# Last pair's token transform: two products over the whole array in place of four on its quarters

## The chip, the core and the metric

The kernel runs on one core of one Trainium2 chip. The metric is the device time of one execution in microseconds (us), the median of several runs. The profiler records one execution; its times are counted from the start of the recorded span.

## What is computed

The input `x` has 2048 tokens of 512 channels. It is normalised over the channels; a spectral filter (a two-dimensional transform, a product with complex weights, the transform back) gives `s`; a token-mixing network (two matrix products over the token axis with a GELU between) and a SiLU give the gate `g`; the result is `x + s * g`.

```
xn = layernorm(x)
s = irfft2(rfft2(xn) * (w_r + 1j * w_i))
u = gelu(einsum("bsd,sf->bdf", xn, w1) + b1)
y = einsum("bdf,fs->bds", u, w2) + b2
return x + s * silu(y.transpose(0, 2, 1))
```

## The kernel before

The tokens are laid out as 128 rows times 16 row blocks. The kernel first normalises, transforms forward, multiplies by the spectral weights and makes the hidden products `h` by `w1` (up to about 200 us); then it runs a loop over `p = 0..7`, each step making the output of two row blocks, `p` and `p + 8`, a *pair*. All of what is described here lies in that loop, and most of it in its last step, `p = 7`.

In a step the tensor engine (PE) makes seven groups of 21 products of 128x128 weights by 256 columns, `products(p, n)` for `n` in `ORDER = (1, 2, 5, 6, 3, 7, 4)`; their left factors are `fa`, `fb`, `fc`, `fd` and their right factors the tiles `w2f`, which ACT and DVE form ahead of time from the loaded tiles `a` and `s`. The sums of the groups lie in PSUM banks 2 to 5. ACT turns them into gates `g`: `gate(g0, ...)` for the first row block, `gate(g1, ...)` for the second. The last group, `n = 4`, completes the left half of the second gate.

Beside that, the transform back over the channels runs on PE (`even_channels`, `odd_channels`, the products of `cd` by `yt`), DVE and ACT fold its output in `unfolded` (tiles `es`, then `y`), and `spectral(p)` makes the transform back over the tokens: `y` (128 rows; two halves of 512 columns, one for each row block) times constants of `cft`, into PSUM banks 0 and 1. It writes

```
for e, cols in enumerate((slice(0, 64), slice(64, P))):
    for r, rows in enumerate((slice(0, 64), slice(64, P))):
        i = e ^ r
        T.matmul(ps[cols, i], cft[rows, cols], y[rows, i], ...)
```

that is, four products of 64 rows by 64 columns of weights, each with 512 moving columns, on the four quarters of the array. They are in plain float32, and every one of them has two records in the trace. The other large products take rounded float32 (`F32R` in the code; the rows call both `f32`) and have one record each.

For `p < 7` the token transform of a pair is run in the next step, among other products. For the last pair it stands in that pair's own step, between `products(7, 7)` and `products(7, 4)` (`k == 5`). Then `finish` multiplies the banks by the gates (DVE, tile `rows`), adds `x` (tile `xr`, loaded earlier) and sends the rows out: `finish(g0, j0, whole)` for the first row block, `finish(g1, j1, right_)` for the right half of the second, and, when the last gate is there, `finish(g1, j1, left_)` in two parts.

Every operation of this loop is recorded by the wrapper `Kept`, so the profile gives them all the same line, L139; they are told apart by their tiles. In this part of the program the engines run their instructions in the order of the code. SP's queue issues the loads; an issue that has to wait for a semaphore holds up those behind it.

Of the kernel before, what the change touches and what calls it, by code (L numbers as in the profile page):

```python
# [9 lines left out]
F32 = mybir.dt.float32  # L10
# [5 lines left out]
P = 128  # L16
# [32 lines left out]
def _k1(lo, hi):  # L49

    (t, h), s = divmod(hi, 2), 2 * lo + hi // 2
    return (64 - s if s else 32) if h else s


def _pairs(lo, t):


    if 2 * lo + t == 0:
        return np.array([[1, 0, 1, 0], [1, 0, -1, 0], [0, 1, 0, 0], [0, 0, 0, 1]], float)
    return np.array([[1, 0, 1, 0], [0, 1, 0, 1], [1, 0, -1, 0], [0, -1, 0, 1]], float)  # L60


def _constants():


    q = np.arange(P)
    a = 2 * np.pi * (np.outer(q, np.arange(32)) % P) / P
    f = np.stack([np.cos(a), np.sin(a)], 2)
    f[0::2, 0, 1], f[1::2, 0, 1] = np.cos(np.pi * q[0::2] / 2), np.sin(np.pi * q[1::2] / 2)
    f = np.concatenate([f[0::2], f[1::2]]).reshape(P, 64)  # L70

    a = 2 * np.pi * (np.outer(2 * np.arange(P) + 1, KD) % (2 * D)) / (2 * D)
    fd = np.stack([np.cos(a), -np.sin(a)])
    fd[1, :, 0] = np.cos(np.pi * np.arange(P))
    fd = fd.reshape(2, P, 2, P).transpose(0, 2, 1, 3).reshape(4, P, P)
    iv = fd.transpose(0, 2, 1) * 2.0 / (D * S)
    iv[0, 0] *= 0.5
    iv[2, 0] *= 0.5  # L80

    g = np.zeros((P, 8, 2, 32, 2))
    back = np.zeros((8, 2, P, 2, 64))
    freq = np.zeros((P, 8, 2), int)
    j = np.arange(16)
    for lo in range(16):
        for hi in range(4):
            k1, (n, l), (t, h) = _k1(lo, hi), divmod(lo, 2), divmod(hi, 2)
            for r in range(16):
                rows = cr, sr = np.arange(16) * 2 + hi * 32, np.arange(16) * 2 + hi * 32 + 1  # L90
                out = np.zeros((2, P))
                if k1:
                    k = [k1 + 128 * r] * 2
                    th = 2 * np.pi * ((j * k[0]) % S) / S
                    out[0, cr], out[0, sr] = np.cos(th), -np.sin(th)
                    out[1, cr], out[1, sr] = -np.sin(th), -np.cos(th)
                elif r == 0:
                    k = [0, S // 2]
                    out[0, cr], out[1, cr] = 1.0, np.cos(np.pi * j)
                else:  # L100
                    k = [128 * r if r < 8 else 64 + 128 * (r - 8)] * 2
                    th = 2 * np.pi * ((j * k[0]) % S) / S
                    out[0, rows[r >= 8]], out[1, rows[r >= 8]] = np.cos(th), -np.sin(th)
                rows = slice(64 * t, 64 * t + 64)

                out[:, rows] = np.einsum("sajb,abhc->shjc", out[:, rows].reshape(2, 2, 16, 2),
                                         _pairs(lo, t).reshape(2, 2, 2, 2)).reshape(2, 64)
                p = [l * 64 + 2 * (h * 16 + r) + c for c in range(2)]
                for s in range(2):
                    g[rows, n, l, h * 16 + r, s] = back[n, t, p[s], 0] = out[s, rows]  # L110
                    freq[p[s], n, t] = k[s]
                if k[0] == k[1]:
                    back[n, t, p[0], 1], back[n, t, p[1], 1] = -out[1, rows], out[0, rows]
                else:
                    back[n, t, p, 1] = out[:, rows]
    freq = freq.reshape(P, 16)


    ft = np.concatenate([np.concatenate([f[:64].T, f[64:].T], 1)] * 2)
    c = {  # L120
        "c_f": f.astype(np.float32),
        "c_ft": np.concatenate([ft, np.array([-1.0, -2.0]) * np.where(q % 2, -1.0, 1.0)[:, None]], 1).astype(np.float32),
        "c_d": fd.transpose(1, 0, 2).astype(np.float32),
        "c_i": iv.transpose(1, 0, 2).astype(np.float32),
        "c_g": g.transpose(1, 0, 2, 3, 4).astype(np.float32),
        "c_h": back.transpose(0, 2, 1, 3, 4).astype(np.float32),
    }
    return c, freq
# [10 lines left out]
        return lambda *args, **kw: self.keep(operation(*args, **kw))  # L139


def spectral_mixer_kernel(tc, x, w1, b1, w2, b2, wk, we, wx, c_f, c_ft, c_d, c_i, c_g, c_h, out):
    nc = tc.nc
    V, A, G, T, SY = nc.vector, nc.scalar, nc.gpsimd, nc.tensor, nc.sync

# [16 lines left out]
    with tc.tile_pool(name="ps", bufs=1, space=PSUM) as psp, ExitStack() as left, ExitStack() as right:  # L162
        ps = psp.tile([P, 8, 512], F32, name="ps")
# [297 lines left out]
        T = Kept(T, keep)  # L461
# [46 lines left out]
        for j in range(NJ):  # L508
# [25 lines left out]
            start, more_stats = j < 3, j + 3 < NJ  # L534
# [38 lines left out]
            if more:  # L573
# [3 lines left out]
                if FIRST <= j < FIRST + NE:  # L577
                    i = j - FIRST
# [206 lines left out]
        for n in range(8):  # L785
            a, b, c, d, e, f = PACE[n]
# [115 lines left out]
        def banks(p):  # L902
            return ps[:, 2 + p % 2, :HD], ps[:, 4, :HD], ps[:, 5, :HD]
# [33 lines left out]
        V, A, SY, G = (Kept(e, keep) for e in (nc.vector, nc.scalar, nc.sync, nc.gpsimd))  # L937
        fp = pool(left, "left", "fin", 1)
# [67 lines left out]
        def spectral(p):  # L1006

            y = ys.pop(p)
            for e, cols in enumerate((slice(0, 64), slice(64, P))):
                for r, rows in enumerate((slice(0, 64), slice(64, P))):  # L1010
                    i = e ^ r
                    T.matmul(ps[cols, i], cft[rows, cols], y[rows, i], start=True, stop=True)

        def gate(g, j, cols, src, scale):
            A.activation(g[:, cols], src, AF.Silu, bias=b2t[:, j:j + 1], scale=scale)

# [18 lines left out]
        yts, ys, pieces = {}, {}, iter(())  # L1035
        last_rows = None

        for p in range(NP):
            j0, j1 = p, p + NP
            more = p + 1 < NP  # L1040
            if p:
                gates[p] = new_gates(p)
            g0, g1 = gates[p]
            bx, by, bz = banks(p)
            slot, plan = SLOTS[min(p, 2) + (not more)]
            gathering = gathered(p)
            for k, n in enumerate(ORDER):
                started = not p and k < 2
                if not started:
                    products(p, n)  # L1050
                if n == 1 and p:
                    p1 = copied(f"p1_{p}", bx, w2p)
                elif n == 5:
                    p5 = copied(f"p5_{p}", bz, fp)
                elif n == 6:
                    v2 = copied(f"v2_{p}", bx, fp)
                elif n == 7:
                    c22 = summed(f"c22_{p}", bx, p5)
                if not started:
                    ready.extend(w for w in [next(wforms, None)] if w is not None)  # L1060
                if n == 2:
                    c11 = summed(f"c11_{p}", by, p1)
                elif n == 6:
                    gate(g0, j0, left_, c11, 1.0)
                elif n == 3:
                    gate(g0, j0, right_, summed(f"c12_{p}", bz, v2), 1.0)
                elif n == 7:
                    gate(g1, j1, right_, c22, -1.0)
                elif n == 4:
                    for cols in (left_,) if more else quarter_rows:  # L1070
                        gate(g1, j1, cols, bx[:, cols], -1.0)
                if not p and k == slot - 1:
                    even_channels(p)
                if k == slot:
                    for part in PARTS[p]:
                        {"S": spectral, "E": even_channels, "O": odd_channels}[part](p - (part == "S"))
                    yts.pop(p)
                    pieces = unfolded(p)
                    if p:
                        for g, j in zip(gates.pop(p - 1), (j0 - 1, j1 - 1)):  # L1080
                            finish(g, j, whole)
                for what in plan.get(k, ""):
                    next(gathering if what == "g" else pieces)
                if more and n == 7:
                    sums_of_blocks()
                if not more and k == 2:
                    xr = [where.tile([P, NH * P], F32, name=f"xr{i}", tag="s1", bufs=1)[:, :D] for i, where in enumerate((w2p, fp))]
                    for to, j in zip(xr, (j0, j1)):
                        for rows, tokens in halved:
                            SY.dma_start(to[rows], x[tokens, j])  # L1090
                if not more and k == 5:
                    spectral(p)
                    last_rows = fp.tile([P, 2, D], F32, name="rows", tag="yt")
                    finish(g0, j0, whole)
                    finish(g1, j1, right_)
# [38 lines left out]
```

## Time and profile before

| | us |
|---|---|
| median of 3 runs | 366.15 |
| lowest and highest of them | 365.76, 366.25 |
| the profiled execution: its own time | 366.07 |
| the profiled execution: its span, first to last instruction | 364.3 |
| PE busy, share of the span | 357.4, 98% |
| DVE busy, share of the span | 306.4, 84% |
| ACT busy, share of the span | 211.1, 58% |
| granted TensorE clock, mean | 0.999 of full speed |

The profiled execution takes 1.8 us more than its span. A row of the timeline gives the start, the length, the engine and the tiles (out<-in) of instructions that are merged into one row where they are alike and follow each other, with their count. PE is the matmul stream, PEld the weight loads, which can run beside it. The ends of matmuls are modelled, and they overlap: what one costs the stream is read from start to start.

### The profile page before, as it was taken

Reading aid. Unit: us, or ns where it says so; the run is one execution under the profiler, and the core shown is the slowest. Engines: PE = TensorE matmul, PEld = TensorE weight load, DVE = VectorE, ACT = ScalarE, POOL = GpSimd, SP = SyncE. Lnnn points to the kernel's source line nnn. Section 1 sums busy time; section 2 is a strip of 40 time slices with the busy share of each in tenths; the row PEclk is TensorE's granted clock in tenths of the full one; section 3 lists DMA queues with packets and bytes.
Section 4 is the critical chain, followed back from the end, with each engine's and each line's share of the span. In section 5 each row is a group of like instructions: output and inputs, shape, how many; then the busy total and the mean of one; then the engine's idle time right before and its main releaser. Section 6 shows DMA issues by size and latency. Waiting matters only on the chain.

```text
span 364.3 us, 8851 instructions
## 1 busy us (share of the span) xinstructions
PE 357.4 (98%) x3476; PEld 310.0 (85%) x3476; DVE 306.4 (84%) x590; ACT 211.1 (58%) x385; POOL 87.2 (24%) x134
## 2 busy tenths in 40 slices
PE   8999999999999999999999999999999999999994
PEld 7788888888777778777888999989898989898993
DVE  4899999967699996999995988687787869696984
ACT  4887788867534426755237875656464545565541
POOL 4233333323222012220120001050403122140330
PEclk9999999999999999999999999999999999999999
DMA  6987899406695697996567298688888989898624
GB/s 207 236 201 197 210 275 305 183 0 161 163 269 191 189 248 183 253 243 186 185 238 154 101 230 176 165 189 201 195 186 212 180 222 158 222 168 228 113 30 87
DMA packets 33294, 68.66 MB, mean 188 GB/s; under 512 B 4613, under 2 KB 19381, under 8 KB 33125
## 3 DMA queue, kind: packets, MB, share of 16 engines
q1 hardware_dynamic: 24276, 42.44, 42.3%
q0 software_dynamic: 8496, 25.01, 32.0%
q10 hardware_dynamic: 480, 0.66, 0.6%
q8 instruction: 27, 0.44, 0.5%
q14 instruction: 15, 0.11, 0.1%
HBM read 59.70 MB, written 8.13 MB: 186 GB/s over the span
## 4 chain that ended last, share of the span: by engine, by line
PE 90%; DVE 3%; DMA 3%; ACT 2%; issue 1%; ACTq 0%; DVEq 0%; SPq 0%
PE ps L139 90%; DMA a<-in_w_dram 2%; DMA w1r<-in_w_dram 1%; DVE es L139 1%; DVE a L836 1%; ACT w2f L139 1%; DVE r L139 0%; ACT fc L363 0%; DVE y L139 0%; DVE c L139 0%; DVE w2f L824 0%; ACT w2f L820 0%; DVE rows L139 0%; ACT u L355 0%; DVE fc L368 0%
## 5 line engine op out<-in xcount | busy, mean ns | idle before, releaser
L139 PE MATMUL ps<-h,w1h 128*128 128x512 f32 x400 | 116.3, 397 | 0.0
L139 PEld LDWEIGHTS ps<-h,w1h 128*128 128x128 f32 x400 | 72.9, 188 | 19.8 <-issue 4.9
L139 PE MATMUL ps<-h,w1l 128*128 128x512 f32 x200 | 67.6, 390 | 0.0
L139 DVE TENSOR_TENSOR w2f<-a,w2f 128x896 fp32r<-128x896 f32 x36 | 39.2, 1090 | 22.1 <-ACT w2f L139 22.1
L139 ACT ACTIVATE w2f<-a 128x896 fp32r<-128x896 f32 x36 | 36.8, 1022 | 13.3 <-PE ps L139 6.7
L139 PEld LDWEIGHTS ps<-h,w1l 128*128 128x128 f32 x200 | 37.5, 188 | 8.1
L139 PE MATMUL ps<-fb,w2f 128*128 128x256 f32 x336 | 41.9, 279 | 0.6 <-DVE c L139 0.6
L139 POOL DMA_DIRECT2D s<-in_w_dram x14 | 18.4, 1312 | 95.8 <-DMA s<-in_w_dram 59.5
L139 PE MATMUL ps<-fa,w2f 128*128 128x256 f32 x336 | 41.2, 277 | 0.0
L139 PEld LDWEIGHTS ps<-fb,w2f 128*128 128x128 f32 x336 | 39.7, 188 | 1.5 <-DVE c L139 1.5
L139 PE MATMUL ps<-fc,w2f 128*128 128x256 f32 x336 | 39.8, 277 | 0.0
L139 PEld LDWEIGHTS ps<-fa,w2f 128*128 128x128 f32 x336 | 39.7, 188 | 0.0
L139 PEld LDWEIGHTS ps<-fc,w2f 128*128 128x128 f32 x336 | 39.0, 188 | 0.0
L155 ACT ACTIVATE w1h<-w1s 128x512 fp32r<-128x512 f32 x26 | 16.2, 631 | 25.0 <-PE ps L139 10.9
L139 POOL DMA_DIRECT2D out_dram<-r x28 | 23.6, 1278 | 28.5 <-DVE r L139 28.5
L667 POOL DMA_DIRECT2D xc<-xc x16 | 9.8, 619 | 69.9 <-ACT xc L665 54.7
L308 POOL TENSOR_TENSOR ey<-t 128x256 f32<-128x256 f32 x16 | 15.7, 979 | 43.8 <-DVE t L306 43.8
L139 ACT ACTIVATE w2f<-s 128x896 fp32r<-128x896 f32 x15 | 15.4, 1023 | 13.6 <-PE ps L139 12.3
L469 DVE TENSOR_TENSOR w1l<-w1r,w1h 128x384 fp32r<-128x384 f32 x32 | 21.3, 670 | 0.0
L139 ACT ACTIVATE g<-c,b2t 128x256 f32<-128x256 f32 x24 | 12.1, 505 | 15.0 <-DVE c L139 15.0
L139 PE MATMUL ps<-fd,w2f 128*128 128x256 f32 x168 | 20.6, 277 | 0.0
L268 ACT ACTIVATE h<-x,nbm,rsm 128x256 f32<-128x256 f32 (+1 forms) x34 | 18.4, 592 | 3.5 <-DVE nbm L263 2.9
(132 smaller groups left out, 606.4 us busy)
## 6 DMA issues: line engine op xcount, KB each, us to landing
a<-in_w_dram SPq DMA_DIRECT2D x22, 448.0 KB, 4.2
wt<-in_wk_dram POOLq DMA_DIRECT2D x16, 512.0 KB, 6.0
s<-in_w_dram SPq DMA_DIRECT2D x16, 448.0 KB, 4.2
s<-in_w_dram POOLq DMA_DIRECT2D x16, 448.0 KB, 6.7
w1s<-in_w_dram SPq DMA_DIRECT2D x52, 128.0 KB, 5.0
w1r<-in_w_dram SPq DMA_DIRECT2D x28, 192.0 KB, 5.5
xc<-xc POOLq DMA_DIRECT2D x16, 256.0 KB, 3.0
out_dram<-in_x_dram SPq DMA_DIRECT2D x4, 960.0 KB, 6.9
```

Source lines behind the costliest of these rows:

```text
L139: return lambda *args, **kw: self.keep(operation(*args, **kw))
L155: return A.activation(hi, src, AF.Copy), V.tensor_sub(lo, src, hi.bitcast(F32))
L268: keep(A.activation(to, v, AF.Identity, bias=m["nb"][:, i], scale=m["rs"][:, i, 1:2]))
L308: G.tensor_add(ey[:, 0::3, :, j], a, b)
L469: keep(V.tensor_sub(dst, src, hi.bitcast(F32)))
L667: keep(G.dma_start(*(v.rearrange("p s t c -> p s (t c)") for v in (there[c::2], here[1 - c::2, ::-1]))))
L836: step(V.tensor_add(cur[name], cur[name], cur[other]))
```

## The change

A constant `c_fs` of two 128x128 blocks is added. Block 0 holds the two diagonal quarters of the constants of `cft` and zeros elsewhere, block 1 the two other quarters. With it `last_spectral` makes each row block's transform as one product of 128 rows, where `spectral` made it as two products of 64 rows. It is used for the last pair alone. The constant is loaded into a new tile `halves` by SP at `p == 2`.

```
+    fs = np.zeros((P, 2, P))
+    for e in range(2):
+        for r in range(2):
+            rows, cols = slice(64 * r, 64 * r + 64), slice(64 * e, 64 * e + 64)
+            fs[rows, e ^ r, cols] = ft[rows, cols]
+        "c_fs": fs.astype(np.float32),
...
+        def last_spectral(p):
+
+            y = ys.pop(p)
+            for i in range(2):
+                T.matmul(ps[:, i], halves[:, i], y[:, i], start=True, stop=True)
...
+                if p == 2 and not k:
+                    halves = fp.tile([P, 2, P], F32, name="halves")
+                    SY.dma_start(halves, c_fs)
                 if not more and k == 5:
-                    spectral(p)
+                    last_spectral(p)
                     last_rows = fp.tile([P, 2, D], F32, name="rows", tag="yt")
                     finish(g0, j0, whole)
                     finish(g1, j1, right_)
```

PE in the last pair, before: the end of the group `n = 7`, the token transform, the start of the group `n = 4`. What stands in brackets are the semaphores that the row waits for (DVE and Activation are those engines' counters, DMAHW those of loads).

```order
L139 MATMUL ps<-fb_2724,w2f_7_4522 128x256
L139 MATMUL ps<-fb_2726,w2f_7_4522 128x256
L139 MATMUL ps<-y_4595,cft 64x512 [waits DVE_49,Activation_49]
L139 MATMUL ps<-y_4595,cft 64x512 x3
L139 MATMUL ps<-fb_1499,w2f_7_4556 128x256 [waits DVE_49]
```

The same place after the change.

```order
L145 MATMUL ps<-fb_2724,w2f_7_4524 128x256
L145 MATMUL ps<-fb_2726,w2f_7_4524 128x256
L145 MATMUL ps<-y_4597,halves 128x512 [waits DMAHW7_49,DVE_49,Activation_49]
L145 MATMUL ps<-y_4597,halves 128x512
L145 MATMUL ps<-fb_1499,w2f_7_4558 128x256 [waits DVE_49]
```

Two instructions stand where four stood, in the same place, and the first waits for the landing of `halves` too.

DVE behind it, before: the products of the banks with the gates and the sums with `x`.

```order
L139 TENSOR_TENSOR rows<-ps,g_4441 128x2x128 [waits PE_49,Activation_49]
L139 TENSOR_TENSOR rows<-ps,g_4441 128x2x128
L139 TENSOR_TENSOR rows<-rows,xr_4527 128x512 [waits DMAHW7_49,DMAHW6_49,DVE_49]
L139 TENSOR_TENSOR rows<-ps,g_4442 128x128 [waits Activation_49]
L139 TENSOR_TENSOR rows<-ps,g_4442 128x128
```

After:

```order
L145 TENSOR_TENSOR rows<-ps,g_4443 128x2x128 [waits PE_49,Activation_49]
L145 TENSOR_TENSOR rows<-ps,g_4443 128x2x128
L145 TENSOR_TENSOR rows<-rows,xr_4529 128x512 [waits DMAHW7_49,DMAHW0_49,DVE_49]
L145 TENSOR_TENSOR rows<-ps,g_4444 128x128 [waits PE_49,Activation_49]
L145 TENSOR_TENSOR rows<-ps,g_4444 128x128
```

The order is the same; the row that begins the second row block waits for PE on its own now, since each of the two products tells of its end, where only the last of the four did.

SP around the new load, before: the loads for pair 3, which are issued during pair 2.

```order
L139 DMA s_11_3194<-in_w_dram 128x896 [waits DMAHW5_49,DMASW0_49]
L139 DMA a_3_3227<-in_w_dram 128x896 [waits DMAHW6_49,DVE_49]
L139 DMA a_3_3254<-in_w_dram 128x896 [waits DVE_49]
L139 DMA s_3_3287<-in_w_dram 128x896 [waits DMAHW0_49,DMASW3_49,DVE_49]
L139 DMA a_11_3318<-in_w_dram 128x896 [waits DMAHW4_49,DMAHW1_49,DVE_49]
```

After:

```order
L145 DMA s_11_3194<-in_w_dram 128x896 [waits DMAHW5_49,DMASW0_49]
L145 DMA a_3_3227<-in_w_dram 128x896 [waits DMAHW6_49,DVE_49]
L145 DMA halves<-in_c_fs_dram 128x256
L145 DMA a_3_3256<-in_w_dram 128x896 [waits DMAHW0_49,DVE_49]
L145 DMA s_3_3289<-in_w_dram 128x896 [waits DMAHW1_49,DMASW3_49,DVE_49]
L145 DMA a_11_3320<-in_w_dram 128x896 [waits DMAHW4_49,DMAHW2_49,DVE_49]
```

The load of `halves` stands between the two loads of `a` and waits for nothing; the load behind it waits for one more counter of loads, and from there on each load takes the next of the eight counters.

## Rows read from the trace of the kernel before

**Rows 1.** The page's head and PE's busy time: us, share, instructions.

```profile
span 364.3 us, 8851 instructions
PE 357.4 (98%) x3476; PEld 310.0 (85%) x3476; DVE 306.4 (84%) x590; ACT 211.1 (58%) x385; POOL 87.2 (24%) x134
```

**Rows 2.** The chain that ended last, its end: start us, us, what.

```profile
219.05 129.17 PE ps L139 x1283
...
354.59 1.21 DVE y L139 x2
...
355.93 3.78 PE ps L139 x29
...
360.13 0.75 DVE rows L139 x3
```

**Rows 3.** Stretches: us, then busy PE, PEld, DVE, ACT, POOL; granted clock, DMA.

```profile
219.10:348.20 129.10, 129.10 (x1287) 123.34 (x1289) 104.32 (x165) 71.15 (x115) 31.90 (x37) 1.00 0.84 183
355.90:359.70 3.80, 3.76 (x29) 2.77 (x29) 2.57 (x7) 0.51 (x1) 0.00 (x0) 1.00 0.29 38
```

**Rows 4.** Timeline of PE around the last token transform: start us, us, what.

```profile
354.74 0.99 PE L139 MATMUL ps<-fb,w2f 128*128 128x256 f32 x7
355.93 0.66 PE L139 MATMUL ps<-y,cft 64*64 64x512 f32 x4 [0.20 <-DVE y L139]
356.38 0.64 PE L139 MATMUL ps<-y,cft 64*64 64x512 f32 x4
356.95 0.39 PE L139 MATMUL ps<-fb,w2f 128*128 128x256 f32 x1
357.18 0.51 PE L139 MATMUL ps<-fb,w2f 128*128 128x256 f32 x3
```

**Rows 5.** Timeline of PEld, the weight loads, at the same place.

```profile
355.90 0.24 PEld L139 LDWEIGHTS ps<-y,cft 64*64 64x64 f32 x8 [0.38 <-issue]
356.95 0.77 PEld L139 LDWEIGHTS ps<-fb,w2f 128*128 128x128 f32 x6 [0.81 <-DVE c L139]
```

**Rows 6.** Timeline of PE at an earlier pair's token transform.

```profile
237.97 0.61 PE L139 MATMUL ps<-y,cft 64*64 64x512 f32 x4
238.41 0.61 PE L139 MATMUL ps<-y,cft 64*64 64x512 f32 x4
```

**Rows 7.** Timeline of PE: full-array products, rounded (w1e, wz) and plain (cd,ey).

```profile
87.93 0.62 PE L139 MATMUL ps<-h,w1e 128*128 128x512 f32 x2
88.39 1.05 PE L139 MATMUL ps<-cd,ey 128*128 128x128 f32 x8
5.47 0.78 PE L139 MATMUL ps<-wz 128*128 128x128 f32 x6
```

**Rows 8.** Groups of matmuls by shape: busy us, mean ns of one, idle before.

```profile
L139 PE MATMUL ps<-h,w1e 128*128 128x512 f32 x72 | 18.1, 398 | 0.0
L139 PE MATMUL ps<-cd,ey 128*128 128x128 f32 x128 | 16.8, 274 | 0.0
L139 PE MATMUL ps<-cf,h 64*64 64x64 f32 x512 | 9.3, 221 | 0.0
L139 PE MATMUL ps<-y,cft 64*64 64x512 f32 x64 | 8.4, 596 | 0.2 <-DVE y L139 0.2
```

**Rows 9.** Timeline of DVE and ACT behind the last token transform.

```profile
357.15 0.76 DVE L139 TENSOR_TENSOR rows<-ps,g 128x256 f32<-128x256 f32 x2 [0.96 <-PE ps L139]
358.55 0.48 DVE L139 TENSOR_TENSOR rows<-ps,g 128x128 f32<-128x128 f32 x2
359.74 0.63 ACT L139 ACTIVATE g<-ps,b2t 128x128 f32<-128x128 f32 x2 [3.00 <-PE ps L139]
360.13 0.55 DVE L139 TENSOR_TENSOR rows<-ps,g 128x128 f32<-128x128 f32 x2 [0.64 <-ACT g L139]
```

**Rows 10.** SP's issues in pair 2, a load of 128 KB, and DVE's first use of these loads.

```profile
248.53 0.33 SPq L139 DMA_DIRECT2D a<-in_w_dram  x1
250.14 0.33 SPq L139 DMA_DIRECT2D a<-in_w_dram  x1
hf<-in_c_h_dram SPq DMA_DIRECT2D x8, 128.0 KB, 3.9
263.02 1.08 DVE L139 TENSOR_TENSOR a<-a,s 128x896 f32<-128x896 f32 x1
```

More of the change, by code (lines that the diff above doesn't have):

```diff
@@ L139, in __getattr__, with spectral_mixer_kernel @@
         return lambda *args, **kw: self.keep(operation(*args, **kw))
-def spectral_mixer_kernel(tc, x, w1, b1, w2, b2, wk, we, wx, c_f, c_ft, c_d, c_i, c_g, c_h, out):
+def spectral_mixer_kernel(tc, x, w1, b1, w2, b2, wk, we, wx, c_fs, c_f, c_ft, c_d, c_i, c_g, c_h, out):
     nc = tc.nc
```

## The prediction, made before the changed kernel was run

> **What bounds the kernel now.** I read the page's head first: PE is busy for 98% of the span [rows 1], so the question is only whether the edited place is on PE's stream, and whether PE's stream sets the end there. The chain of waits says so twice. From 219.05 to 348.22 us it is PE alone [rows 2], and the table by stretches has PE busy for 129.10 of 129.10 us there [rows 3]: nothing that DVE, ACT or a load does in that stretch is late. At the end the chain goes over: DVE makes `y`, PE runs 29 records from 355.93 to 359.71, ACT makes the last gate, DVE makes the last rows from 360.13 on, the last transfers go out [rows 2, 9]. The 29 records are the eight of the token transform and the 21 of the group `n = 4`. So the token transform of the last pair lies on the path itself: it starts when `y` is there (PE idles 0.20 us for it), and everything behind it, `n = 4`, gate, rows, transfer, follows in line. A nanosecond more or less on PE between 355.90 and the start of `n = 4` is one at the end of the span.
>
> **What is removed: four quarter products.** Each has two records. The first four start at 355.93, the second four at 356.38, and the first record of `n = 4` starts at 356.95 [rows 4]. The four of a round start together, one on each quarter: four products of 512 columns cost what one costs. From round to round an earlier, undisturbed block takes 238.41 - 237.97 = 0.44 (0.432 before rounding, and the same in the blocks of the five pairs that follow) [rows 6]; at the granted clock of 1.00, the level of 2.4 GHz [rows 3], 0.43 us is two cycles for each of 512 columns and a few more.
>
> The start of `n = 4` is not free either. Its first weights are loaded only at 356.95, when the quarter products are nearly through [rows 5]; its first record is 0.39 long, against about 0.28 in the run of the group before, and its second starts at 357.18. Seven records of that group take 0.99, so one costs (0.99 - 0.28) / 6 = 0.118 [rows 4]. Counted back from the second record, the group begins in effect at 357.18 - 0.12 = 357.06: 0.11 us go into an uncovered weight load. The block thus holds the stream from the load at 355.90 to 357.06, 1.16 us.
>
> **What is added: two products over the whole array.** They start from the same wait, at 355.90. Their first weights are not covered, as those of `n = 4` were not: 0.11, effective start 356.01. Two products have four records of 512 columns, which can't go beside each other, since each takes all rows and all columns of the array. The unknown is what a record of 512 columns in plain float32 costs on the whole array: no row of before has one.
>
> - From below, the rounded product of the same shape: two in 0.62 with 0.39 for the last one, 0.23 each [rows 7, 8]. Four: 0.92.
> - From the quarters: 0.432 each, four 1.73.
> - From above, the plain product of 128 columns over the whole array, taken four times as long: eight in 1.05, so (1.05 - 0.27) / 7 = 0.111 each [rows 7], 0.445 for 512 columns. Four: 1.78.
>
> I take the quarters' 0.432. The row of 128 columns doesn't decide it, since the rounded product of 128 columns costs the same 0.10 [rows 7], so that the load of 128 columns of weights limits both. What speaks for two cycles a column is the length of the records, though their ends are modelled: plain ones take 221 ns for 64 columns and 596 for 512 on the quarters, 0.84 ns a column, and 128 columns over the whole array take 274, which lies on that line (221 + 64 x 0.84 = 275) [rows 8]. The rows thus tie the two cycles to the type and not to the quarters.
>
> The Trainium skill ("FP8 and Floating Point Precision", TensorE Precision Notes) gives true float32 four passes through the array. By that the two products take 8 passes of 512 columns, 8 x 512 / 2.4 GHz = 1.71 us as an estimate; by the row of the rounded product they take 0.92. On the quarters the trace agrees with the page (two records, each as long as two passes); no row shows it for the whole array.
>
> The weights of the second to fourth records, and those of `n = 4`, should load under the 0.43 of the record before: plain records of 128 columns keep a spacing of 0.111 with a load in each [rows 7], so a load takes a quarter of a record.
>
> **Sum.** 356.01 + 4 x 0.432 = 357.74 for the effective start of `n = 4`, against 357.06: **0.68 us later.** The bounds are 356.01 + 0.92 = 356.93 (0.13 earlier) and 356.01 + 1.78 = 357.79 (0.73 later), and, with a load uncovered in each of the last three records and in `n = 4`, 0.44 more (below).
>
> The Trainium skill ("TensorEngine Tiling (Array Packing)", Key Properties) says that changing the tiling mode drains the engine, which speaks for this change: it removes two such changes. The rows show 0.20 us of idling ahead of the block that waits for `y` anyway, and 0.11 behind it; that 0.11 is in the sum, and a drain beyond it would have to show as more.
>
> **What follows on the path.** `n = 4` is unchanged and takes the same 21 records. ACT has idled 3.00 us before the last gate, and DVE 0.64 us before the last rows [rows 9], so both still wait for PE, and gate, rows and transfer move by the same 0.68.
>
> **What is beside the path.** DVE's first rows start at 357.15, right behind the four products. Now they wait for the first product alone; its second record starts at 356.44 and by its modelled length of 0.59 ends at 357.03, as the four did at 357.02. No gain. The second row block's rows start at 358.55 and will wait for the second product, which ends by the same length at 357.30 + 0.59 = 357.89: 0.6 us of margin. The early transfers stay where they are, and an earlier one would gain nothing.
>
> **The load of `halves`.** It stands on SP between the loads of 248.53 and 250.14, where SP has 1.28 us free, and an issue takes 0.33 [rows 10]. A load of 128 KB lands in 3.9, 100 us before it is wanted. It shares the transfer engines with the next load of `a`, whose first user on DVE is at 263.02 [rows 10], more than 8 us after it lands; PE has no gap to grow. Cost nothing; if that cover were gone, the time its bytes take at 183 GB/s [rows 3], 0.7 us. The added wait of the first product for that landing is met long before; its handling lies within the step from `y` to the first product, about 0.14, so its price is 0 to 0.14, and I take 0 because nothing else is queued on PE at that point but this product and `n = 4`.
>
> **The number.** The profiled execution took 366.07, of which 364.3 is span and 1.8 lies around it unchanged: 366.07 + 0.68 = 366.75. It stands 0.08 below the median of the runs shown, so against 366.15 the forecast is **366.8 us**, 0.19% more. About 0.2%, 0.73 us, is what a measurement of this kernel can tell from no change; three runs here lie within 0.49 us of each other. The forecast thus sits just inside that bound.
>
> **Rivals.**
>
> *The whole array takes a column a cycle.* Then the two cycles on the quarters come from two column halves sharing one stream of rows, and a record costs 0.23: 0.13 us earlier, **366.0 us**. For it: the change is then a gain, and no start-to-start row excludes it. Against it: the lengths by type. Such a column a cycle is what the Trainium skill ("TensorE: Matmul & The Clock Gate", Back-to-back issue gap) gives for a matmul without naming a type; the rounded rows agree, the plain ones on quarters don't.
>
> *The weight loads are not covered.* The four records each bring a load of 128 columns, and `n = 4` another; if plain weights can't be loaded under a running product of the same kind, each costs 0.11 as that of `n = 4` does today: 0.68 + 4 x 0.11 = 1.12, **367.3 us**. It decides from the first uncovered load on, which makes 0.79 us, over 0.2%. For it: the load of 356.95 was uncovered, behind plain products. Against it: there the engine changed from quarters to whole array, and the plain 128-column records, load and all, keep 0.111.
>
> *The new load disturbs.* It delays a load of `a` or `s` that somebody waits for, up to 0.7 on top of 0.68, **367.5 us**. Against it: the margin of 8 us.
>
> **How the numbers follow.** The forecast has a chance of 0.80, the column a cycle 0.08, the uncovered loads 0.08, the disturbing load 0.04. The forecast's own value can be off by 0.1 (a record at 0.445, the third wait) and the measurement by 0.25: its 0.80 splits into 0.45 within 0.2%, 0.34 slower, 0.01 faster. The column a cycle gives 0.06 same and 0.02 faster, the two others 0.11 slower and 0.01 same. Together: faster 0.03, same 0.52, slower 0.45. The range of 366.4 to 367.3 leaves out the first rival and the tails.
>
> **What would show it.** Right: four records of 128x512 by `halves`, 0.43 from start to start; the first record of `n = 4` of 0.28 and not 0.39, with its weight load ahead of it, near 357.74; DVE's first rows still near 357.15, the last gate near 360.4; SP's load near 248.9 and PE still without a gap from 219 to 348. Wrong: records 0.23 or 0.54 apart, gaps between PE's records where none were, or DVE rather than PE ahead of the last gate.

## The result, and the profile after

| | before | after |
|---|---|---|
| median of 14 runs each, us | 366.02 | 366.68 |
| lowest to highest | 365.31 to 367.37 | 366.05 to 368.04 |
| the profiled execution: span | 364.3 | 364.9 |

The ratio is 1.0019, with a 95% interval of 1.0010 to 1.0027: the change makes the kernel 0.66 us slower, and the interval lies on both sides of the 0.2% that was called the bound of no change.

The timeline of PE around the last token transform after the change, which answers to [rows 4]; each row is a record that ran at a chosen instant (start us, us, what):

```profile
355.83 0.67 PE L145 MATMUL ps<-y,halves 128*128 128x512 f32 x1 [0.15 <-issue]
...
356.33 0.59 PE L145 MATMUL ps<-y,halves 128*128 128x512 f32 x1
...
357.19 0.59 PE L145 MATMUL ps<-y,halves 128*128 128x512 f32 x1
357.22 0.68 PE L145 MATMUL ps<-fb,w2f 128*128 128x256 f32 x1
...
357.74 0.52 PE L145 MATMUL ps<-fb,w2f 128*128 128x256 f32 x3
```

And its weight loads (PEld), which answer to [rows 5]:

```profile
355.80 0.30 PEld L145 LDWEIGHTS ps<-y,halves 128*128 128x128 f32 x2 [0.33 <-issue]
...
356.76 0.19 PEld L145 LDWEIGHTS ps<-y,halves 128*128 128x128 f32 x1 [0.24 <-issue]
357.19 0.19 PEld L145 LDWEIGHTS ps<-fb,w2f 128*128 128x128 f32 x1 [0.24 <-issue]
```

Four records of 512 columns start at 355.83, 356.33, 356.76 and 357.19 (the third is read from the weight load of the fourth, which starts with it): 0.43 from start to start, and 0.50 for the first, whose weight load is not covered. Every further load starts with the record before it and is over long before the next; the `[0.24 <-issue]` is the loader being idle, not late. The group `n = 4` has its second record at 357.74, so it begins in effect at 357.74 - 0.12 = 357.62. From the first weight load at 355.80 the block takes 1.82 us, where it took 1.16 [rows 4, 5]. That is 0.66 more.

DVE and ACT behind it, which answer to [rows 9]:

```profile
357.03 0.76 DVE L145 TENSOR_TENSOR rows<-ps,g 128x256 f32<-128x256 f32 x2 [0.90 <-PE ps L145]
...
358.43 0.48 DVE L145 TENSOR_TENSOR rows<-ps,g 128x128 f32<-128x128 f32 x2
...
360.69 0.55 DVE L145 TENSOR_TENSOR rows<-ps,g 128x128 f32<-128x128 f32 x2 [1.31 <-ACT g L145]
...
360.29 0.63 ACT L145 ACTIVATE g<-ps,b2t 128x128 f32<-128x128 f32 x2 [3.61 <-PE ps L145]
```

DVE's first rows still start 1.23 us behind the first weight load (1.25 before), and the second row block's do not wait. But the last gate is at 360.29, where it was at 359.74, and DVE idles 1.31 us ahead of the last rows, where it idled 0.64. What PE lost is idle time for the others, and the end moved by it. The chain of waits shows the same; its end, answering to [rows 2]:

```profile
355.83 4.44 PE ps L145 x25
...
360.29 0.38 ACT g L145
...
360.69 0.75 DVE rows L145 x3
```

PE's piece grew from 3.78 to 4.44 us, by 0.66; the pieces behind it are what they were.

The new load on SP, answering to [rows 10]:

```profile
247.84 0.33 SPq L145 DMA_DIRECT2D a<-in_w_dram  x1
248.22 0.52 SPq L145 DMA_DIRECT2D halves<-in_c_fs_dram  x1
249.45 0.33 SPq L145 DMA_DIRECT2D a<-in_w_dram  x1
```

It fits between the two loads, as it was placed in the order. PE has no gap behind it; the row of the same stretch as in [rows 3]:

```profile
219.10:348.20 129.10, 129.10 (x1283) 123.33 (x1286) 104.50 (x166) 70.42 (x115) 31.88 (x37) 1.00 0.84 184
```

### The profile page after: what moved, and what is told of

The parts are those of the page before. It is cut to its first block, busy times and chain, and to the rows that moved or that the text cites. A ratio compares the mean times of both kernels' runs of the same rounds, so it can differ in the third digit from the quotient of the medians.

```text
span 364.9 us, 8846 instructions
## 1 busy us (share of the span) xinstructions
PE 358.8 (98%) x3472; PEld 311.6 (85%) x3472; DVE 306.5 (84%) x590; ACT 211.1 (58%) x385; POOL 87.1 (24%) x134
## 4 chain that ended last, share of the span: by engine, by line
PE 97%; DMA 1%; DVE 1%; issue 0%; ACT 0%; DVEq 0%
PE ps L145 97%; DMA x<-in_x_dram 1%; DVE rows L145 0%; DVE stm L250 0%; DVE h L278 0%; ACT g L145 0%; DVE tm L235 0%; ACT sdm L229 0%; DVEq L1145 0%; DVE mvm L226 0%; DVE r0m L234 0%; DVE rsm L236 0%; DVE v2m L227 0%; DVE v2m L228 0%; DVEq L475 0%
```

## The experiments

**One part undone: the load and the wait stay, the products go back to the quarters.** The quarters of `halves` that are not zero are the constants of `cft`, so the four small products can take their weights there.

```
-            for i in range(2):
-                T.matmul(ps[:, i], halves[:, i], y[:, i], ...)
+            for e, cols in enumerate((slice(0, 64), slice(64, P))):
+                for r, rows in enumerate((slice(0, 64), slice(64, P))):
+                    i = e ^ r
+                    T.matmul(ps[cols, i], halves[rows, i, cols], y[rows, i], ...)
```

> The changed kernel with one part undone: the new constant is loaded and waited for as in the changed kernel, but the last pair's transform is again four products of 64x64, whose weights are the quarters of the new tile that hold the constants. Theory (the cost is the shape of the products): as the kernel before, 366.0 us, ratio 1.000; the eight records on the quarters take 0.43 from round to round. Rival (the cost is the new load, or the wait for it): as the changed kernel, 366.7 us, ratio 1.0019.

Measured: 366.03 us, ratio 1.0000 (0.9988 to 1.0011). The timelines of PE and of PEld:

```profile
356.22 1.09 PE L145 MATMUL ps<-y,halves 64*64 64x512 f32 x8
357.24 0.97 PE L145 MATMUL ps<-fb,w2f 128*128 128x256 f32 x6
```

```profile
356.19 0.24 PEld L145 LDWEIGHTS ps<-y,halves 64*64 64x64 f32 x8 [0.32 <-issue]
```

From the first weight load to the first record of `n = 4` it is 1.05 us, as before (356.95 - 355.90). The load of `halves` and the wait for it cost nothing in this stretch, and nothing in the whole time to within the 0.4 us of its interval; the products' shape is what costs.

**The same form in all eight pairs.**

```
-                        {"S": spectral, ...
+                        {"S": last_spectral, ...
-                if p == 2 and not k:
+                if p == 0 and not k:
```

> The changed form in all eight pairs in place of the last alone (the constant is loaded in pair 0). Theory (PE's stream is longer by four serial records of 0.43 against two rounds): in the six or seven pairs where the stream is bound by PE each transform costs 0.62 to 0.73 more, as in the last one, so 366.0 + 8 x 0.66 = 371.3 us, between 370.3 and 371.8; the first weight load may be covered or not. Rival (the cost is one of the end of the program, of the way from the last product to the last transfer): the other seven hide, 366.7 to 367.0 us.

Measured: 375.21 us, ratio 1.0246 (1.0220 to 1.0272). The rival fell: the earlier pairs do not hide it. But it is 9.2 us and not 5.3, so my number fell too, and the trace had to say why.

**The same form in pairs 3, 4 and 5 alone**, which shows a changed pair beside an unchanged one in one trace.

```
-                        {"S": spectral, ...
+                        {"S": last_spectral if 3 <= p - 1 <= 5 else spectral, ...
-                    last_spectral(p)
+                    spectral(p)
```

> The whole-array form in pairs 3, 4 and 5 alone, the last pair and the others on quarters; the load in pair 2. Theory (PE's stream): each of the three costs what e2's trace shows between the products around it, 0.86 us (0.85 for the block, 0.10 for its first weight load, less 0.10 behind it), so 366.0 + 2.6 = 368.6 us with the spacing unchanged. If the whole-array products bring the 0.118 spacing to the groups behind them, 0.66 more for each of pairs 4, 5 and 6: 370.6 us. Rival (only the end of the program matters): 366.0 us.

Measured: 370.80 us, ratio 1.0137 (1.0124 to 1.0150): the second of the three cases. Its timeline of PE, around the first changed pair:

```profile
292.86 2.54 PE L145 MATMUL ps<-fb,w2f 128*128 128x256 f32 x21
295.33 0.69 PE L145 MATMUL ps<-cd,yt 64*64 64x64 f32 x32
295.95 1.98 PE L145 MATMUL ps<-y,halves 128*128 128x512 f32 x4
...
298.58 2.72 PE L145 MATMUL ps<-fb,w2f 128*128 128x256 f32 x21
301.14 2.63 PE L145 MATMUL ps<-fd,w2f 128*128 128x256 f32 x21
...
316.70 1.98 PE L145 MATMUL ps<-y,halves 128*128 128x512 f32 x4
```

The same stretch of the kernel before, pairs 1 and 2:

```profile
237.46 0.69 PE L139 MATMUL ps<-cd,yt 64*64 64x64 f32 x32
237.97 1.04 PE L139 MATMUL ps<-y,cft 64*64 64x512 f32 x8
...
239.86 2.63 PE L139 MATMUL ps<-fb,w2f 128*128 128x256 f32 x21
242.32 2.54 PE L139 MATMUL ps<-fd,w2f 128*128 128x256 f32 x21
...
257.21 1.04 PE L139 MATMUL ps<-y,cft 64*64 64x512 f32 x8
```

Two things are to be seen. First the place itself: from the small products `cd,yt` to the next group it is 298.58 - 295.33 = 3.25 us with the whole array and 239.86 - 237.46 = 2.40 on the quarters, 0.85 more. Of these, 0.11 lie ahead of the transform: behind other products on quarters, the one on quarters starts 0.51 behind the first `cd,yt`, the one on the whole array 0.62. Behind its start it is 0.74 more, where the last pair had 0.66. Three such pairs make 2.6. Second, what stands behind: a group of 21 takes 2.54 ahead of the first whole-array transform and 2.63 behind it, in every group up to the last pair (the group right behind a transform takes 0.09 more in either case: 2.72 here, 2.63 at 239.86 in the kernel before). That is 0.118 us a product in place of 0.113, 0.094 a group, 0.66 for the seven groups of a pair. From one changed transform to the next it is 316.70 - 295.95 = 20.75 us, against 257.21 - 237.97 = 19.24 before: 1.51, which is 0.85 + 0.66. Behind the third changed transform only five groups stand before the next one, early in the last pair, and the groups behind that have 0.118 in the kernel before as well. So the sum is 3 x 0.85 + 19 x 0.094 = 4.3. Measured are 370.80 - 365.92 = 4.9, with an interval from 4.5 to 5.5; the few tenths between are not explained. The eight pairs of the run before come near in the same way: their trace has 0.118 in all the groups of pairs 3 to 6. Seven transforms at 0.85, the last at 0.66 and 33 groups at 0.094 (from the last group of pair 2 to the fourth of the last pair) make 9.7, measured 9.2.

**Where the tile lies: the changed kernel with the load in pair 0.** The run of all pairs had moved the tile and its load, too.

```
-                if p == 2 and not k:
+                if p == 0 and not k:
```

> The changed kernel with the new tile made and loaded in pair 0 in place of pair 2, as in e2, the products as in the changed kernel. If e2's wider spacing of PE's products (0.118 in place of 0.113 us in pairs 3 to 6, 0.66 a pair) comes from where the tile lies or when it is loaded: 366.7 + 4 x 0.66 = 369.3 us and 0.118 in its trace. If it comes from the whole-array products of the earlier pairs: 366.7 us, 0.113 from pair 2 or 3 on.

Measured: 366.65 us, ratio 1.0023 (1.0013 to 1.0033), with 0.113 from pair 3 on: as the changed kernel. Neither the place nor the time of the load matters; the wider spacing came with the whole-array transforms of the earlier pairs.

**The type of the products.** The whole-array form with rounded float32, one record for each product. Not shown: the tile `yr` takes the buffer that `rows` had, and `rows` that of `y`.

```
-                    halves = fp.tile([P, 2, P], F32, name="halves")
-                    SY.dma_start(halves, c_fs)
+                    loaded = fp.tile([P, 2, P], F32, name="loaded", tag="c", bufs=2)
+                    SY.dma_start(loaded, c_fs)
+                    halves = fp.tile([P, 2, P], F32R, name="halves")
+                    A.activation(halves, loaded, AF.Copy)
...
+            if p == NP - 1:
+                y = fp.tile([P, 2, 2, 2, P], F32R, name="yr", tag="yt")
```

> The changed form with rounded float32 for the constant and for the last pair's y (y goes to a tile of its own; the precision of this pair's transform is lower). Theory (a record of plain float32 takes two cycles a column, twice for each product, because of its type): two records of 128x512, 0.23 apart; block of 0.11 + 0.46 = 0.57 against 1.16 before and 1.82 in the changed kernel: 0.6 faster than before, 365.4 us. Rival (the whole array or the write to PSUM sets 0.43 a record, whatever the type): 0.11 + 0.86 = 0.97, 0.2 faster than before, 365.8 us; DVE's first rows would begin earlier in both.

Measured: 372.24 us, ratio 1.0145 (1.0107 to 1.0184). Both expected times fell, for a reason of my own making. The timeline of ACT in pair 2, that of PE, and a row of stretches behind the wait (columns as in [rows 3], the granted clock third from the end):

```profile
252.73 0.42 ACT L145 ACTIVATE halves<-loaded 128x256 fp32r<-128x256 f32 x1 [6.92 <-DMA loaded<-in_c_fs_dram]
```

```profile
254.98 4.19 PE L145 MATMUL ps<-fa,w2f 128*128 128x256 f32 x21 [3.08 <-ACT p L145]
```

```profile
257.00:259.00 2.00, 2.00 (x12) 2.00 (x11) 1.41 (x3) 0.46 (x2) 0.00 (x0) 0.50 0.84 231
```

ACT stood 6.92 us with the copy at the head of its queue, waiting for the load; behind it was `p`, for which PE waited 3.08. That wait is not all that it cost: behind it the granted clock was 0.50, the level of 1.2 GHz, from 257 to 259 us, and the group took 4.19 us where it takes 2.63 at 1.00. And the groups keep the wider spacing, which they had before, up to the last pair. A load costs nothing where only a queue that can wait has to wait for it; it costs the path where a busy engine meets it first.

**The same, with the copy three groups later.**

```
+                if p == 2 and k == 3:
+                    halves = fp.tile([P, 2, P], F32R, name="halves")
+                    A.activation(halves, loaded, AF.Copy)
```

> As e3, with the copy that rounds the constants three groups later on ACT, so that ACT no longer waits for their load (in e3 it did, and PE stood for 3.4 us behind it; the precision of the last pair's transform is lower again). Theory (a plain float32 record is long because of its type): the block from y to the group n=4 is 0.57 against 1.16 before, 0.6 faster than before, 365.4 us, if PE's products of 256 columns keep the 0.113 spacing that they have from pair 3 on in the changed kernel; where they keep the 0.118 of e3 in all of pairs 3 to 6, 0.66 a pair on top: 368.0 us. Rival (what e3 lost had another cause than ACT's wait and the spacing): 370 us or more.

Measured: 365.61 us, ratio 0.9996 (0.9986 to 1.0005). The timeline of PE, its weight loads and DVE there:

```profile
355.10 0.40 PE L145 MATMUL ps<-fb,w2f 128*128 128x256 f32 x2
355.53 0.42 DVE L145 TENSOR_TENSOR c<-ps,p 128x256 f32<-128x256 f32 x1
355.61 0.30 PEld L145 LDWEIGHTS ps<-yr,halves 128*128 128x128 f32 x2 [0.32 <-DVE yr L145]
355.61 0.73 PE L145 MATMUL ps<-yr,halves 128*128 128x512 f32 x2
...
356.07 0.53 PEld L145 LDWEIGHTS ps<-fb,w2f 128*128 128x128 f32 x4 [0.17 <-issue]
356.18 0.52 PE L145 MATMUL ps<-fb,w2f 128*128 128x256 f32 x3
```

The two records and the load ahead of them take 356.18 - 355.61 = 0.57 us, as the theory had it, down to the second digit: a record of the rounded type costs 0.23 on the whole array and one of the plain type 0.43, so the length belongs to the type. The whole kernel gained 0.31 by its medians, though; the interval holds a gain of 0.5 at most, not the 0.6 of the stretch, and it holds no gain as well. The profiled execution did gain it: its loop, from the first group to the end of the last, takes 358.81 - 218.17 = 140.64 us, and that of the run with the quarters of `halves`, whose spacing falls in the same pair, 359.98 - 218.75 = 141.23. Why the medians show less stays open. What comes up behind is seen in the run of both, below.

**The columns in DVE's order, on the quarters** (the kernel before, with nothing of the change). DVE writes `y` in two instructions, 1.28 us together, and each fills half of the columns.

```
+            y = ys.pop(p).rearrange("p i (h q c) -> p i q h c", h=2, q=2)
+            to = ps[:, :2].rearrange("p i (h q c) -> p i q h c", h=2, q=2)
+            for q in range(2):
...
+                        T.matmul(to[cols, i, q], cft[rows, cols], y[rows, i, q], ...)
```

> The kernel before with the last pair's transform on the quarters in two steps of 256 columns, in the order in which DVE makes y: the first step needs only the first of DVE's two writes of y. Theory (PE idles 0.20 us for the second write): the first step starts right behind the group n=7, the block of PE from the end of n=7 to the start of n=4 is 0.1 to 0.2 shorter, less some 0.05 for two more rounds: 365.85 to 366.0 us, ratio 0.9995 to 1.000. Rival (the idle time is PE's change to the quarters, not the wait): it stays, and two more rounds cost 0.05 to 0.1: 366.1 us.

Measured: 365.64 us, ratio 0.9988 (0.9976 to 1.0000). The timeline of PE:

```profile
354.78 0.99 PE L144 MATMUL ps<-fb,w2f 128*128 128x256 f32 x7
355.70 1.09 PE L144 MATMUL ps<-y,cft 64*64 64x256 f32 x16
356.72 1.45 PE L144 MATMUL ps<-fb,w2f 128*128 128x256 f32 x10
```

From the last record of `n = 7` (355.77 - 0.28 = 355.49) to the first of `n = 4` it is 1.23 us; before it was 356.95 - (355.73 - 0.28) = 1.50 [rows 4]. The quarter products start 0.21 behind the last record of `n = 7` instead of 0.48. The stretch is 0.27 shorter, more than the 0.1 to 0.2 of the theory. So PE's idle time was the wait for `y`, and two more rounds cost no time (1.02 from the first record to `n = 4` in both). This version is ahead of the kernel before by 0.12%, at the edge of its interval, and with that ahead of the changed one.

**Both: rounded, and the columns in order.**

> e6 (whole array, rounded float32 for the constants and the last y, so a lower precision of this pair's transform) with the columns in two steps in DVE's order, as in e4. Theory: both gains lie on PE between the group n=7 and the group n=4 and add up; that stretch, 1.61 before and 0.97 in e6's trace, is 0.2 shorter, 0.75: 365.1 us, ratio 0.9976. Rival (e6 measured half of what its trace gains, so something behind PE takes over): no faster than e6, 365.5 us.

Measured: 365.43 us, ratio 0.9988 (0.9977 to 0.9999). Its timeline:

```profile
355.53 0.40 PE L145 MATMUL ps<-fb,w2f 128*128 128x256 f32 x2
...
355.65 0.68 PEld L145 LDWEIGHTS ps<-yr,halves 128*128 128x128 f32 x4
355.77 0.77 PE L145 MATMUL ps<-yr,halves 128*128 128x256 f32 x4
355.97 0.42 DVE L145 TENSOR_TENSOR c<-ps,p 128x256 f32<-128x256 f32 x1
...
356.51 0.65 PEld L145 LDWEIGHTS ps<-fb,w2f 128*128 128x128 f32 x5 [0.18 <-issue]
```

The theory of two gains that add up fell, and the rival held. PE's last record of the transform starts at 355.77 + 0.77 - 0.28 = 356.26 and holds the stream for some 0.12, but the weights of `n = 4` are not loaded before 356.51: that group goes on in the bank that DVE still has to read, in `c<-ps,p`, which ends at 355.97 + 0.42 = 356.39. The group begins in effect 0.11 behind that load, at 356.62, 0.97 us behind the last record of `n = 7` at 355.65. In the rounded run before, the same stretch is 356.18 - 355.22 = 0.96, and there, too, the load stands 0.12 behind the end of that sum (356.07, and 355.53 + 0.42 = 355.95): that run had just reached this bound. It is the next bound at this place: once the transform takes less than DVE's sum, the sum takes over.

**Both kernels once more, unchanged**, to see what of the traces belongs to one execution.

> The kernel before, unchanged, profiled once more. In its first trace PE's products of 256 columns go 0.118 us apart up to pair 1 and 0.113 apart from pair 2 to pair 6; in the changed kernel's from pair 3 to 6. If that pair is a matter of the single execution: another onset is possible here. If it is fixed by the program: 0.113 from pair 2 on, as before. Time 366.0 us.

> The changed kernel, unchanged, profiled once more. If the pair in which the spacing falls from 0.118 to 0.113 us is fixed by the program: pair 3 again. If it is a matter of the execution: possibly another. In either case four records by the new tile 0.43 apart, and 1.8 us from the first weight load to the effective start of the group n=4. Time 366.7 us.

Measured: 365.90 and 367.89 us, one execution each. The kernel before again, around the transform that stands ahead of the last group of pair 2:

```profile
257.06 1.04 PE L139 MATMUL ps<-y,cft 64*64 64x512 f32 x8
...
258.95 2.63 PE L139 MATMUL ps<-fb,w2f 128*128 128x256 f32 x21
261.41 2.54 PE L139 MATMUL ps<-fd,w2f 128*128 128x256 f32 x21
```

In its first trace the groups of 2.54 begin at 242.32, here at 261.41, one pair later, with the same program. In both traces of the changed kernel they begin in pair 3 (at 261.51 and 262.69). In its last pair the second trace again has records 0.43 apart and a block of 1.82 us (356.97 to 358.79). At the first pair, where the loop starts, the changed kernel has, in the second trace:

```profile
217.75 0.69 PE L145 MATMUL ps<-cd,yt 64*64 64x64 f32 x32
219.53 2.74 PE L145 MATMUL ps<-fb,w2f 128*128 128x256 f32 x21 [1.08 <-DVE c L145]
```

And in the first:

```profile
217.72 0.69 PE L145 MATMUL ps<-cd,yt 64*64 64x64 f32 x32
218.35 2.74 PE L145 MATMUL ps<-fb,w2f 128*128 128x256 f32 x21
```

In the second trace the group starts 1.78 us behind the start of the products `cd,yt`, in the first 0.63, without a wait. The difference, 1.15, is nearly all that the second execution took longer (367.89 against 366.72). The kernel before varies in the same way: 219.05 - 217.81 = 1.24 in its first trace, with 0.55 of waiting, and 218.25 - 217.53 = 0.72 in its second. By the chain of waits it is a load of `a` that ACT and DVE wait for at this place, issued at 210.5; it lands 5.5 us later in the first trace of the kernel before, and 6.05 in the second of the changed one. Both effects move the end by some tenths of a microsecond up to one and more. Neither has to do with the change, since each differs between two executions of one program.

## Why the prediction was right

- **The place on the path.** Right. PE's piece of the chain grew by 0.66, and gate, rows and transfer moved with it.
- **The quarters go beside each other, the whole-array products don't.** Right: two rounds before, four records after, and undoing this part alone brought 366.03.
- **The unknown, a record of 512 columns over the whole array.** The value taken from the quarters, 0.432, was measured as 0.43. The bound from the rounded type, 0.23, was what the rounded type costs and not the plain one; with it falls the rival of a column a cycle. The Trainium skill ("FP8 and Floating Point Precision", TensorE Precision Notes) had four passes for true float32; two products in four records of 0.43 agree with that.
- **Weight loads covered but for the first.** Right: the load of each further record runs inside the record before. The rival of uncovered loads fell.
- **The sum.** 1.84 for the block was predicted, 1.82 measured; 0.68 later, and 0.66 by the stretch and by the medians. That the medians agree to the second digit is luck, since their interval runs from 0.37 to 0.99 us. Nothing beyond the 0.11 of the uncovered load was saved by no longer going to the quarters and back: the sum came out without such a term.
- **The added wait, taken at nothing.** Nearly. The step from `y` to the first weight load is 0.12 before (DVE's two writes end at 354.50 + 1.28 = 355.78, the load starts at 355.90) and 0.08 after (354.44 + 1.28 = 355.72, and 355.80), though there are more counters to wait for. The bounds were put at 0 to 0.14; it fell just below.
- **The load of `halves`.** Right, and two runs bear it out, the one with the quarters of `halves` and the one with the load in pair 0. That the cover matters was seen when ACT waited for the same load, and PE 3.08 us for ACT.
- **What the changed profile would show.** One item missed: the first record of `n = 4` was to be 0.28 long. It is 0.68, since with its weights loaded early it is recorded from 357.22 on, while the last transform record still streams. The length of one matmul record is no measure of its cost; start to start is.
- **Not seen.** That the groups behind a whole-array transform in the middle pairs go at the wider spacing. It doesn't bear on the last pair, where only one group follows (0.118 in both kernels' traces), and so not on the number; the forecast of the eight-pair run failed mostly by it.

## What to carry to other kernels

Products that each fill a quarter of the array cost one product's time together; joining them with zeros into whole-array products adds the columns up and buys nothing, unless the join comes with a type that needs fewer records. Whether the rounded type would do on the quarters, no run here shows. Before such a trade, find the record of the same type and take it start to start. And before a small difference between two traces is put down to a change, profile the unchanged kernel twice: here the first waits of the loop and the spacing of one pair each move the end by as much as the change does.

## What was not expected of the hardware

The same product, 128x128 by 256 columns of rounded float32, has two spacings at the same granted clock: 0.113 and 0.118 us from start to start, 2.54 and 2.63 us for a group of 21. A group keeps one of them. In every trace here the spacing changed only across a block of other products, but the form of the block alone does not say which way. In the middle pairs it became 0.113 behind transforms on quarters, and 0.118 behind the first whole-array transform. In the last pair most traces go back to 0.118 behind a transform on quarters. But the run with all eight pairs changed becomes narrow there, behind a whole-array transform and small products:

```profile
356.23 1.88 PE L145 MATMUL ps<-y,halves 128*128 128x512 f32 x4
358.04 1.78 PE L145 MATMUL ps<-cd,yt 64*64 64x64 f32 x40
...
362.05 2.54 PE L145 MATMUL ps<-fb,w2f 128*128 128x256 f32 x21
```

And the first rounded run has 0.118 all through pairs 3 to 6, with every transform there on quarters. In which pair it first becomes 0.113 differs between two executions of one program. It is worth 0.66 us a pair, as much as the change, and the cause was not settled: the type, the tiles and their places are the same in both, and no wait shows in either. Without it the two first traces mislead: they lie within 0.1 us of each other at 348 us only because the kernel before started its loop 0.70 later (219.05 against 218.35) and had one more pair of the narrow spacing.
